# Attention into mixture-of-experts on one core: list operands by nine token tiles, wider routing steps, later weight rounding, and a sooner split of every second pair's outputs

## The chip, the cores and the metric

The kernel runs on 1 core of one Trainium2 chip, in one launch. The metric is device time in microseconds. Before the change it is 1155.81 us, the median of three runs (1155.4 to 1158.08).

## The reference

```
# q, k, v: 8 batches x 8 heads x 1152 x 64; q is averaged over pairs of positions -> 576 queries
q_pool = q.reshape(B, H, S // 2, 2, D).mean(axis=3)
scores = (1 / sqrt(D)) * q_pool @ k^T           # 576 x 1152 for each head
attn   = softmax(scores)                        # row maxima subtracted
x      = (attn @ v), heads side by side         # 4608 tokens x 512
logits = x @ w_gate + modality_bias[modality_id]        # 8 experts
e_idx  = argmax(logits);  gate = softmax(logits)[e_idx] # one expert for each token
out[t] = gate[t] * (relu(x[t] @ w1[e]) @ w2[e])         # 512 -> 1024 -> 512
```

All inputs and outputs are f32. The kernel splits f32 values into a high and a low 16-bit part and sums the products of the parts.

## The kernel before, in words

**Pairs.** The 64 heads are taken as 32 pairs (two batches of one head index, 128 partitions). `attention` runs 32 x 18 steps; `now[0]` is the step, and a pair's steps are its places 0 to 17. The order of TensorE, ScalarE, VectorE and GpSimd is the order of issue, written out by hand: in each step the letters of `ORD` advance generators for scores (`s`), value products (`v`) and the maxima of the next pair (`M`, `X`), `J` advances the logits' generators and `F` runs what `later(n, ...)` put off by n steps; `ends(t)` then runs what `later_end` and `go`/`at` put at the step's end. SyncE's queue, which issues most DMAs, is ordered by the scheduler of the framework instead.

**A pair's path.** `load_kq`, `split_q`, `split_qh`, `split_hi`, `split_lo` bring q and k of a pair two pairs ahead and split them (GpSimd and ScalarE). `maxpass` multiplies q and k (L778, L786), VectorE reduces each bank to maxima (L779, L787) out of three banks; at the end VectorE makes the row's maxima `m` (L749), TensorE turns them (L753), VectorE writes `mr` (L762), and a DMA (L763) puts `mr` into row 64 of `B2`. The scores' second matmul (L844) reads `B2`. ScalarE exponentiates each of four tiles of a unit (L845); the low words of the exponentials are made in two pieces, columns 0 to 1152 on ScalarE (L826) and 1152 to 1728 on VectorE (L828), as the `LOWS` tables say ('A' ScalarE, 'D' VectorE). Value products (L896 to L898) add into one bank for each head, and `evac` (L914 to L919) empties it; the second head's is emptied at place 4 of the next pair.

**Splitting the outputs.** `evac` then puts off `split_x` by `XD` = 5 steps (place 9): ScalarE makes `xh` (L862). `XL` = 3 steps later (place 12) VectorE makes `xl` (L872). For every second pair (odd p) a DMA transpose of two pairs' columns is issued after each (L880, SyncE), and the logits' job is put on a list that is looked at at place 8.

**Routing.** Nine token tiles of 128 (two batches, 8 pairs) are a group; there are four. When a group's logits are summed, `route` runs as the generator at the head of `side`, one piece at a time: the number that it yields is the number of steps to the next piece. It finds the maximum, the expert, the gate and each token's position within its expert. Groups 0, 1 and 2 are routed from pairs 9, 17 and 25 on, group 3 beside the experts.

**First list.** After group 2, `first_list` plans the six first blocks of 256 tokens (`first_blocks`), finds each token's place (`place`) and makes the list of tokens for each block by matmuls of one-hot operands (`operands`, `listing`, `indices`). At step 557, just before pair 31, `early` drains what is left of it, gathers the first block's tokens (GpSimd) and loads its weights; `T_W0` and `T_W1` say at which places of pair 31 the four pieces are loaded and rounded (L1432).

**Experts.** 18 blocks of 256 tokens and one of 128: two matmul stages with weights split into high and low parts. `beside()` advances group 3's logits, its `route` and `other_list` once for each twelfth or sixth matmul, whatever they yield; sixteen times a block. After block 4 the rest is drained.

Of the kernel before, what the change touches and what calls it, by code (L numbers as in the profile page):

```python
# [42 lines left out]
T_LIST = -127  # L43
RS = 2
SLOW_P = 1
# [72 lines left out]
W1D = 0  # L118
T_W1 = (6, 4, 10, 11)
E1 = 1  # L120
# [40 lines left out]
class Router:  # L161
# [11 lines left out]
    def setup(self, ids, w_gate, bias):  # L173
# [20 lines left out]
        nc.gpsimd.memset(self.on, 1.0)  # L194
        self.ie = self.iota("ie", E)
        self.lane16 = con.tile([P, P], BF16, name="lane16")
        nc.gpsimd.tensor_copy(self.lane16, self.iota("lane", P))
# [75 lines left out]
    def route(self, g, eng):  # L273

        nc, sm = self.nc, self.sm
        while self.added[g] < H // 2:
# [15 lines left out]
        yield RS + 1  # L292
# [16 lines left out]
        yield RS  # L309
# [11 lines left out]
        eng.dma_start(out=self.xs[g * NT * P:(g + 1) * NT * P, DM:XW].rearrange("(t p) d -> p t d", p=P), in_=gt)  # L321
        yield RS
# [3 lines left out]
        nc.tensor.matmul(pr[:, 0:NT], self.up, oh16, start=True, stop=False, skip_group_check=True)  # L326
        for s in range(NT):
            nc.tensor.matmul(pr[:, s + 1:], self.on, oh16[:, s:s + 1].broadcast_to([P, NT - s, E]), start=False, stop=s == NT - 1,
                             skip_group_check=True)
# [5 lines left out]
        self.base = nb  # L335
        yield RS
        nc.gpsimd.tensor_tensor(pos, pos, oh, op=ALU.mult)
        yield RS
        nc.vector.tensor_reduce(self.pos[:, ts], pos, op=ALU.add, axis=AX.X)
# [29 lines left out]
    def first_blocks(self):  # L369

        nc, sm = self.nc, self.sm
        full = self.con.tile([P, E], F32, name="full")
        self.up_to(self.base, full)
        yield
        cum = self.running(full.unsqueeze(1), "cumA")[:, 0]
        yield
        left = sm.tile([P, E], F32, name="left")
        nc.vector.tensor_scalar(left, cum[:, 0:E], -1.0, float(NA), op0=ALU.mult, op1=ALU.add)
        nc.vector.tensor_single_scalar(left, left, 0.0, op=ALU.max)
        self.na = self.con.tile([P, E], F32, name="na")  # L380
        nc.vector.tensor_tensor(self.na, full, left, op=ALU.min)
        yield
        nc.vector.tensor_single_scalar(cum, cum, float(NA), op=ALU.min)
        self.cumA = cum
        yield
        self.ownA = self.owners(cum, NA, "A")

# [37 lines left out]
    def place(self, nt, late):  # L425
# [11 lines left out]
        def pick(o, of):  # L437

            nc.vector.tensor_tensor(w, oh, be(of), op=ALU.mult)
            yield  # L440
            nc.vector.tensor_reduce(o, w, op=ALU.add, axis=AX.X)
            nc.vector.tensor_single_scalar(o, o, float(TB), op=ALU.mult)
            yield
# [5 lines left out]
        if late:  # L449
            yield from pick(ok, self.done)  # L450
            nc.vector.tensor_tensor(ok, self.pos[:, 0:nt], ok, op=ALU.is_ge)
            more = new("more")
            yield from pick(more, self.half)
            nc.vector.tensor_tensor(more, more, ok, op=ALU.mult)
            nc.vector.tensor_tensor(row, row, more, op=ALU.add)
        yield
        nc.vector.tensor_tensor(ok, self.pos[:, 0:nt], lim, op=ALU.is_ge if late else ALU.is_lt)
# [4 lines left out]
        lo = sm.tile([P, NTT], I32, name="loi")[:, 0:nt]  # L462
        nc.vector.tensor_single_scalar(lo, ri, P - 1, op=ALU.bitwise_and)
        nc.vector.tensor_single_scalar(ri, ri, 7, op=ALU.logical_shift_right)
# [3 lines left out]
        nc.vector.tensor_copy(self.hi, ri)  # L468
        nc.vector.tensor_single_scalar(self.hi, self.hi, -float(2 * T // P), op=ALU.add)

    def operands(self, g, n, out):

        nc, sm = self.nc, self.sm
        for q in range(3):
            ts = slice(g * NT + 3 * q, g * NT + 3 * q + 3)
            ol = sm.tile([P, 3, P], BF16, name=f"ol{q}", bufs=1 + self.lag)
            nc.vector.tensor_tensor(ol, self.lo[:, ts].unsqueeze(2).broadcast_to([P, 3, P]), self.lane16.unsqueeze(1).broadcast_to([P, 3, P]),
                                    op=ALU.is_equal)
# [3 lines left out]
            nc.vector.tensor_tensor(o, self.hi[:, ts].unsqueeze(2).broadcast_to([P, 3, n]), self.col[:, 0:n].unsqueeze(1).broadcast_to([P, 3, n]),  # L482
                                    op=ALU.is_equal)
            nc.vector.tensor_tensor(r[:, :, 0], o, self.tile1[:, ts].unsqueeze(2).broadcast_to([P, 3, n]), op=ALU.mult)
            nc.vector.tensor_scalar(r[:, :, 1], o, self.part, None, op0=ALU.mult)
            out.append((ol, r))
            yield SLOW

    def listing(self, groups, n, acc):

        nc, ops = self.nc, []
        for g in range(groups + self.lag):
            if g < groups:
                ops.append([])
                yield from self.operands(g, n, ops[g])
            elif self.lag:
                for _ in range(self.ll):
                    yield
            g -= self.lag
            if g >= 0:  # L500
                pm = self.pm(4)[:, 0:2 * n].rearrange("p (w n) -> p w n", w=2)
                for t in range(NT):
                    ol, r = ops[g][t // 3]
                    nc.tensor.matmul(pm, ol[:, t % 3], r[:, t % 3], start=t == 0, stop=t == NT - 1)
# [40 lines left out]
def attention(tc, ctx, att, ident, npairs, xpool, on_two, on_split, on_scale, jobs, side, set_pm, started, ahead, hip):  # L545
# [260 lines left out]
    def scores(p, j, r):  # L806
# [9 lines left out]
        s["P", j, r] = (word(F16, 1), Pl, i % NR)  # L816
        lows = LOWS_LAST if p == npairs - 1 else LOWS_LIST if p >= P_LIST else LOWS if p else LOWS0
        lows = lows[i % len(lows)]
# [86 lines left out]
    def evac(p, j, xp):  # L905
# [585 lines left out]
```

## Time and profile before

| | |
|---|---|
| median of the runs | 1155.81 us |
| profiled execution, its time | 1161.75 us |
| its span | 1160.0 us |
| granted TensorE clock, mean | 0.992 of full speed |
| TensorE busy | 1108.3 us (96%) |
| VectorE busy | 983.8 us (85%) |
| ScalarE busy | 920.6 us (79%) |
| GpSimd busy | 414.1 us (36%) |

The attention stage fills about the first 754 us, the experts the rest. A busy TensorE is not TensorE at its peak, since matmuls overlap and their ends are modelled; so lengths of equal pieces of work, and waits, are compared. In the tables of waits a line reads: engine, what waited and its line, what released it, then the sum in us, how often, and the longest. In a timeline a line gives the start, the length, the engine, the line, the operation, out<-in with shapes, how many are merged, and in brackets the idle time before it and what ended that.

### The profile page before, as it was taken

To read this page: it belongs to the slowest core of one execution; us is meant where nothing else is said; L and a number is where in the kernel's file an instruction comes from. 1 tells how busy PE (TensorE), PEld (TensorE's weight loads), DVE (VectorE), ACT (ScalarE), POOL (GpSimd) and SP (SyncE) were. 2 spreads that over 40 slices of the span, in tenths; PEclk is the share of its full clock that TensorE was granted. 3 is DMA by queue.
4 is the path that set the end of the run, shared out by engine and by line. 5 is a ranking of instruction groups with operands and counts; after the bars stand their busy time and mean duration, and the time that the engine had idled before them with its cause. 6 is when DMAs were issued, how large, how long until landed. Compare 5 with 4: busy or idle time off the path is not lost. (4 is left out here: it accounts for less than half of the span.)

```text
span 1160.0 us, 36631 instructions
## 1 busy us (share of the span) xinstructions
PE 1108.3 (96%) x14963; PEld 814.4 (70%) x14963; DVE 983.8 (85%) x2023; ACT 920.6 (79%) x1469; POOL 414.1 (36%) x394
## 2 busy tenths in 40 slices
PE   5999999999999999999999999899999999999995
PEld 2777777777777777777777677767676676666763
DVE  6999999999999999999999999688987667566661
ACT  5999999989999998999999999766656656565561
POOL 7853434444443444435344441123112221211211
PEclk8999999999999999999999999999999999999998
DMA  7766867866868768668678463699899999999980
GB/s 227 203 174 164 185 166 166 190 168 165 174 160 203 162 165 192 158 164 188 173 160 185 131 142 82 178 275 275 260 278 297 300 268 274 277 286 279 264 239 22
DMA packets 175569, 232.66 MB, mean 201 GB/s; under 512 B 92351, under 2 KB 126799, under 8 KB 175392
## 3 DMA queue, kind: packets, MB, share of 16 engines
q1 hardware_dynamic: 169254, 210.45, 70.3%
q0 software_dynamic: 6128, 19.78, 6.3%
q8 instruction: 119, 1.95, 0.7%
q14 instruction: 58, 0.48, 0.1%
q10 hardware_dynamic: 10, 0.00, 0.0%
HBM read 146.11 MB, written 19.18 MB: 142 GB/s over the span
## 5 line engine op out<-in xcount | busy, mean ns | idle before, releaser
L845 ACT ACTIVATE Pe<-psc 128x432 int32<-128x432 f32 x768 | 379.3, 526 | 49.9 <-PE psc L844 40.6
L779 DVE TENSOR_REDUCE mp<-pm 128x1 f32<-128x512 f32 x566 | 372.8, 684 | 23.3 <-PE pm L778 17.0
L896 PE MATMUL xp<-VH,Pe 128*128 128x65 f16 x2880 | 372.8, 194 | 0.0
L898 PE MATMUL xp<-VS,Pl 128*128 128x65 f16 x2880 | 372.2, 193 | 0.4 <-DVE Pl L828 0.4
L897 PE MATMUL xp<-vl,Pe 128*128 128x64 f16 x2880 | 371.0, 192 | 0.0
L897 PEld LDWEIGHTS <-Pe 128*128 128x128 f16 x2880 | 267.9, 98 | 87.6 <-issue 0.2
L844 PE MATMUL psc<-B 65*128 65x432 f16 (+2 forms) x1152 | 306.0, 288 | 8.9 <-DMA B<-mr 8.9
L896 PEld LDWEIGHTS <-Pe 128*128 128x128 f16 x2880 | 272.2, 98 | 54.8 <-issue 17.7
L843 PE MATMUL psc<-B 128*128 128x432 f16 (+2 forms) x1152 | 305.5, 287 | 3.4 <-ACT Pe L845 3.1
L898 PEld LDWEIGHTS <-Pl 128*128 128x128 f16 x2880 | 266.7, 97 | 0.6 <-DVE Pl L828 0.5
L826 ACT ACTIVATE Pl<-Pe 128x1152 f16<-128x1152 uint16 x196 | 223.3, 1140 | 6.2
L778 PE MATMUL pm<-hi,QB 128*128 128x512 f16 x566 | 214.6, 381 | 9.4 <-DVE mp L779 8.8
L731 POOL TENSOR_SCALAR VH<-rawv,sc 128x512 f16<-128x512 f32 (+1 forms) x60 | 103.5, 1735 | 173.9 <-PE psc L844 76.8
L644 POOL TENSOR_TENSOR lo<-rawk,hi 128x576 f16<-128x576 f32 (+1 forms) x68 | 87.6, 1291 | 186.3 <-ACT hi L628 147.4
L1230 PE MATMUL ph<-xpart,w1h 128*128 128x256 f16 x544 | 148.3, 273 | 0.1
L1232 PE MATMUL ph<-xpart,w1l 128*128 128x256 f16 x544 | 148.3, 273 | 0.0
L1231 PE MATMUL ph<-xpart,w1h 128*128 128x256 f16 x544 | 148.3, 273 | 0.0
L844 PEld LDWEIGHTS <-B 65*128 65x128 f16 x1152 | 113.3, 98 | 29.3 <-issue 5.1
L843 PEld LDWEIGHTS <-B 128*128 128x128 f16 x1152 | 113.0, 98 | 9.3 <-issue 4.0
L1236 DVE SCALAR_TENSOR_TENSOR hl<-ph,hh 128x512 f16<-128x512 f32 x72 | 49.6, 689 | 77.9 <-ACT hh L1235 62.3
L1235 ACT ACTIVATE hh<-ph 128x512 f16<-128x512 f32 x72 | 43.0, 597 | 88.5 <-PE ph L1232 80.3
L1278 PE MATMUL po<-w2h,hl 128*128 128x512 f16 x296 | 112.2, 379 | 0.0
(264 smaller groups left out, 1909.2 us busy)
## 6 DMA issues: line engine op xcount, KB each, us to landing
w2r<-in_w_dram SPq DMA_DIRECT2D x76, 512.0 KB
w1r<-in_w_dram SPq DMA_DIRECT2D x72, 512.0 KB
rawv<-in_att_dram SPq DMA_DIRECT2D x32, 576.0 KB
B<-hi SPq DMA_DIRECT2D x128, 144.0 KB
rawq<-in_att_dram SPq DMA_DIRECT2D x31, 576.0 KB
rawk<-in_att_dram SPq DMA_DIRECT2D x31, 576.0 KB
B<-qh SPq DMA_DIRECT2D x128, 72.0 KB
B<-lo SPq DMA_DIRECT2D x64, 144.0 KB
```

Source lines behind the costliest of these rows:

```text
L778: nc.tensor.matmul(pm, QB[p % 2][:, u], s["hi"][:, t * 512:(t + 1) * 512], start=True, stop=True)
L779: nc.vector.tensor_reduce(mp[:, u, t:t + 1], pm, op=ALU.max, axis=AX.X)
L826: nc.scalar.activation(low, rest, AF.Copy, scale=LOW)
L843: nc.tensor.matmul(o, b1[:, ks], b1[:, qs], start=True, stop=False, skip_group_check=True)
L844: nc.tensor.matmul(o, b2[:, ks], b2[:, qs], start=False, stop=True, skip_group_check=True)
L845: nc.scalar.activation(Pe[:, D + x0:D + x1], pt, AF.Exp, scale=1.0 / 16)
L896: nc.tensor.matmul(out, Ph[:, qs], vh[:, c, j, 0:D + 1], start=c == 0 and g == 0, stop=False, skip_group_check=True)
L897: nc.tensor.matmul(out[:, 0:D], Ph[:, qs], vl[:, c, j], start=False, stop=False, skip_group_check=True)
L898: nc.tensor.matmul(out, Pl[:, qs], vs[:, c, j, 0:D + 1], start=False, stop=c == NKC - 1, skip_group_check=True)
L1230: nc.tensor.matmul(o, hi[:, c, fs], xh[:, :, c], start=c == 0, stop=False)
L1231: nc.tensor.matmul(o, hi[:, c, fs], xl[:, :, c], start=False, stop=False)
L1232: nc.tensor.matmul(o, lo[:, c, fs], xh[:, :, c], start=False, stop=c == 3)
```

## The change

It has five parts. The split of an odd pair's outputs is put off by 2 steps instead of 5, for all but the last pair. `route` yields `RS[g]` steps (4, 4, 2, 2) instead of 2, three single steps are added to it, the expert's key is made in one operation with a table shifted by -8 (`ieE`), the one-hot is written as bf16 only, and three small operations go from VectorE to GpSimd. `first_blocks` and `place` are cut into more pieces, with one step between pieces in `first_blocks` and `PL` = 2 in `place`, and the multiplication by the block's size is fused. The operands of a list are made for a group of nine tiles in five pieces instead of three times two. The low words of pairs 28 to 30 are made on VectorE again where one in three was on ScalarE. The first two weight pieces of the first block are rounded at places 7 and 6 instead of 6 and 4.

```diff
-RS = 2
+PL = 2
+RS = (4, 4, 2, 2)
-P_LIST = 26
-LOWS_LIST = (((0, 1152, 'A', 2), (1152, 1728, 'D', 3)), ((0, 1152, 'A', 2), (1152, 1728, 'D', 3)), ((0, 1152, 'A', 2), (1152, 1728, 'A', 3)))
+P_LIST = {26: 0, 27: 0}
+LOWS_LIST = [tuple(((0, 1152, 'A', 2), (1152, 1728, e, 3)) for e in x) for x in ('DDA', 'DA', 'A')]
-T_W1 = (6, 4, 10, 11)
+T_W1 = (7, 6, 10, 11)
...
     def route(self, g, eng):
...
-        yield RS
+        yield rs
         nc.scalar.activation(w, lg, AF.Exp)
-        nc.vector.tensor_single_scalar(w2, lg, 0.0, op=ALU.is_ge)
         key = big[1][:, 0]
-        nc.vector.scalar_tensor_tensor(key, w2, -float(E), be(self.ie), op0=ALU.mult, op1=ALU.add)
+        nc.vector.scalar_tensor_tensor(key, lg, 0.0, be(self.ieE), op0=ALU.is_ge, op1=ALU.mult)
         kmin = sm.tile([P, NT], F32, name="kmin")
         nc.vector.tensor_reduce(kmin, key, op=ALU.min, axis=AX.X)
-        yield RS
-        oh = big[1][:, 1]
+        yield rs
+        oh = sm.tile([P, NT, E], BF16, name="oh16")
         nc.vector.tensor_tensor(oh, key, bc(kmin), op=ALU.is_equal)
-        oh16 = sm.tile([P, NT, E], BF16, name="oh16")
-        nc.vector.tensor_copy(oh16, oh)
-        nc.vector.tensor_single_scalar(self.exp[:, ts], kmin, float(E), op=ALU.add)
-        yield RS
+        yield 1
+        nc.gpsimd.tensor_scalar(self.exp[:, ts], kmin, float(E), None, op0=ALU.add)
+        yield rs
         sx = sm.tile([P, NT], F32, name="sx")
         nc.vector.tensor_reduce(sx, w, op=ALU.add, axis=AX.X)
-        nc.vector.tensor_single_scalar(sx, sx, EPS, op=ALU.add)
...
         nc.vector.tensor_reduce(ts2[:, 0:1], self.scales[g].bitcast(F32), op=ALU.max, axis=AX.X)
-        nc.vector.tensor_single_scalar(ts2[:, 0:1], ts2[:, 0:1], 1.0 / XSC, op=ALU.mult)
+        yield 1
+        nc.gpsimd.tensor_scalar(sx, sx, EPS, None, op0=ALU.add)
+        nc.gpsimd.tensor_scalar(ts2[:, 0:1], ts2[:, 0:1], 1.0 / XSC, None, op0=ALU.mult)
+        yield 1
         nc.vector.reciprocal(ts2[:, 1:2], ts2[:, 0:1])
...
     def operands(self, g, n, out):
-        for q in range(3):
-            ts = slice(g * NT + 3 * q, g * NT + 3 * q + 3)
-            ol = sm.tile([P, 3, P], BF16, name=f"ol{q}", bufs=1 + self.lag)
...
-            yield SLOW
-            o = sm.tile([P, 3, n], F32, name=f"o{n}")
-            r = sm.tile([P, 3, 2, n], BF16, name=f"r{n}_{q}", bufs=1 + self.lag)
...
+        ts = slice(g * NT, (g + 1) * NT)
+        r = sm.tile([P, 2, NT, n], BF16, name=f"r{n}", bufs=1 + self.lag)
+        ols = [sm.tile([P, 3, P], BF16, name=f"ol{q}", bufs=1 + self.lag) for q in range(3)]
...
+        rows(0)
+        yield SLOW
+        o = sm.tile([P, NT, n], F32, name=f"o{n}")
+        nc.vector.tensor_tensor(o, self.hi[:, ts].unsqueeze(2).broadcast_to([P, NT, n]), self.col[:, 0:n].unsqueeze(1).broadcast_to([P, NT, n]),
+                                op=ALU.is_equal)
+        yield SLOW
+        rows(1)
+        yield SLOW
+        nc.vector.tensor_tensor(r[:, 0], o, self.tile1[:, ts].unsqueeze(2).broadcast_to([P, NT, n]), op=ALU.mult)
+        nc.vector.tensor_scalar(r[:, 1], o, self.part, None, op0=ALU.mult)
+        yield SLOW
+        rows(2)
+        yield SLOW
...
     def first_list(self):
         for _ in self.first_blocks():
-            yield 2
+            yield 1
         for _ in self.place(3 * NT, False):
-            yield 2
+            yield PL
...
-            later(XD, lambda: split_x(p, x2))
+            later(2 if p % 2 and p < npairs - 1 else XD, lambda: split_x(p, x2))
```

## Rows read from the trace of the kernel before

**Rows 1.** Waits of TensorE, the whole span.

```profile
PE psc L844 <- DMA B<-mr: 8.9, 10, 1.6
PE pm L778 <- DVE mp L779: 8.8, 15, 1.1
```

**Rows 2.** Windows by pair, 9, 10, 14, 15, 26 to 29; columns: PE, PEld, DVE, ACT, POOL.

```profile
232.33:256.95 24.62, 23.62 (x416) 18.28 (x415) 23.98 (x64) 22.24 (x38) 10.71 (x14) 1.00 0.62 167
256.95:278.74 21.79, 20.95 (x357) 16.09 (x355) 20.88 (x48) 20.09 (x35) 10.46 (x9) 1.00 0.80 174
...
346.55:367.51 20.96, 20.95 (x360) 16.18 (x359) 20.20 (x45) 19.98 (x36) 9.04 (x7) 1.00 0.90 202
367.51:390.48 22.97, 22.97 (x404) 17.77 (x403) 22.00 (x48) 21.82 (x37) 9.78 (x9) 1.00 0.55 149
...
618.14:640.05 21.91, 21.48 (x367) 16.51 (x365) 21.39 (x60) 20.96 (x37) 10.91 (x10) 1.00 0.84 187
640.05:666.80 26.75, 24.41 (x409) 18.37 (x406) 26.15 (x65) 24.06 (x40) 9.52 (x8) 1.00 0.48 130
666.80:689.24 22.44, 21.03 (x361) 16.20 (x359) 22.05 (x55) 21.25 (x37) 9.84 (x8) 1.00 0.73 146
689.24:713.24 24.00, 22.99 (x400) 17.64 (x399) 23.37 (x56) 22.44 (x38) 7.95 (x6) 1.00 0.35 89
```

**Rows 3.** Timeline of SyncE's queue in pair 20.

```profile
487.64 5.91 SPq L880 DMA_TRANSPOSE xt<-x  x2
493.65 0.80 SPq L763 DMA_DIRECT2D B<-mr  x1
```

**Rows 4.** Timeline of VectorE in pair 20.

```profile
490.37 0.27 DVE L762 TENSOR_SCALAR mr<-pm 9x128 f16<-9x128 f32 x1
```

**Rows 5.** Timeline of TensorE at the starts of pairs 0 and 21.

```profile
18.01 0.52 PE L844 MATMUL psc<-B 65*128 65x432 f16 x1 [1.14 <-DMA B<-mr]
...
497.63 0.34 PE L844 MATMUL psc<-B 65*128 65x432 f16 x1 [1.56 <-DMA B<-mr]
```

**Rows 6.** Timeline of VectorE in pair 14, places 11 and 12.

```profile
354.32 0.18 DVE L749 TENSOR_REDUCE m<-mp 128x9 f32<-128x27 f32 x1
354.42 0.81 DVE L872 SCALAR_TENSOR_TENSOR x<-x,sc,x 128x576 f16<-128x576 f32 x1
355.14 0.45 DVE L828 TENSOR_SCALAR Pl<-Pe 128x576 f16<-128x576 uint16 x1
```

**Rows 7.** Timeline of TensorE in pair 14.

```profile
354.57 0.27 PE L753 MATMUL pm<-ident,m 128*9 128x128 f32 x1
```

**Rows 8.** Timeline of GpSimd in pair 14.

```profile
350.87 1.60 POOL L644 TENSOR_TENSOR lo<-rawk,hi 128x576 f16<-128x576 f32 x1 [2.68 <-ACT hi L628]
```

**Rows 9.** Timelines of VectorE and of GpSimd in pair 25.

```profile
613.36 0.63 DVE L305 TENSOR_TENSOR wide<-wide,kmin 128x72 f32<-128x72 f32 x1
...
613.22 1.56 POOL L731 TENSOR_SCALAR VH<-rawv,sc 128x512 f16<-128x512 f32 x1 [6.17 <-PE pm L778]
```

**Rows 10.** Groups by line and shape, VectorE: the lists' operands; busy us, mean ns.

```profile
L477 DVE TENSOR_TENSOR ol<-lof,lane 128x384 bf16<-128x384 bf16 x21 | 11.6, 550 | 0.0
...
L485 DVE TENSOR_SCALAR r<-o,part 128x114 bf16<-128x114 f32 x12 | 3.9, 325 | 0.0
...
L482 DVE TENSOR_TENSOR o<-hif,col 128x114 f32<-128x114 f32 x12 | 3.3, 272 | 0.0
L485 DVE TENSOR_SCALAR r<-o,part 128x36 bf16<-128x36 f32 x9 | 2.2, 243 | 0.0
...
L482 DVE TENSOR_TENSOR o<-hif,col 128x36 f32<-128x36 f32 x9 | 1.7, 187 | 0.0
```

**Rows 11.** The same view: the low words on VectorE.

```profile
L828 DVE TENSOR_SCALAR Pl<-Pe 128x576 f16<-128x576 uint16 x176 | 91.8, 522 | 2.7 <-ACT Pe L845 1.4
```

**Rows 12.** Timeline of ScalarE in pair 31.

```profile
735.98 1.06 ACT L1432 ACTIVATE w1h<-rawk 128x1024 f16<-128x1024 f32 x1 [2.48 <-DMA rawk<-in_w_dram]
```

**Rows 13.** Timeline of TensorE in pair 31.

```profile
737.51 0.28 PE L843 MATMUL psc<-B 128*128 128x288 f16 x1 [2.22 <-ACT Pe L845]
```

More of the change, by code (lines that the diff above doesn't have):

```diff
@@ L195, in setup @@
         self.ie = self.iota("ie", E)
+        self.ieE = self.iota("ieE", E, base=-E)
         self.lane16 = con.tile([P, P], BF16, name="lane16")
@@ L273, in route @@
     def route(self, g, eng):
-        nc, sm = self.nc, self.sm
+        nc, sm, rs = self.nc, self.sm, RS[g]
         while self.added[g] < H // 2:
@@ L289, in route @@
         nc.gpsimd.tensor_tensor(w, w, w2, op=ALU.add)
-        yield RS
+        yield rs
         nc.gpsimd.tensor_tensor(lg, lg, w, op=ALU.add)
-        yield RS + 1
+        yield rs + 1
         mx = sm.tile([P, NT], F32, name="mx")
@@ L321, in route @@
         eng.dma_start(out=self.xs[g * NT * P:(g + 1) * NT * P, DM:XW].rearrange("(t p) d -> p t d", p=P), in_=gt)
-        yield RS
+        yield rs
         for _ in range(self.ll - 1):
@@ L325, in route @@
         pr = self.pm(4)[:, 0:(NT + 1) * E].rearrange("p (t e) -> p t e", e=E)
-        nc.tensor.matmul(pr[:, 0:NT], self.up, oh16, start=True, stop=False, skip_group_check=True)
+        nc.tensor.matmul(pr[:, 0:NT], self.up, oh, start=True, stop=False, skip_group_check=True)
         for s in range(NT):
-            nc.tensor.matmul(pr[:, s + 1:], self.on, oh16[:, s:s + 1].broadcast_to([P, NT - s, E]), start=False, stop=s == NT - 1,
+            nc.tensor.matmul(pr[:, s + 1:], self.on, oh[:, s:s + 1].broadcast_to([P, NT - s, E]), start=False, stop=s == NT - 1,
                              skip_group_check=True)
@@ L335, in route @@
         self.base = nb
-        yield RS
+        yield rs
         nc.gpsimd.tensor_tensor(pos, pos, oh, op=ALU.mult)
-        yield RS
+        yield rs
         nc.vector.tensor_reduce(self.pos[:, ts], pos, op=ALU.add, axis=AX.X)
@@ L372, in first_blocks @@
         full = self.con.tile([P, E], F32, name="full")
-        self.up_to(self.base, full)
+        i = sm.tile([P, E], I32, name="cnti")
+        nc.vector.tensor_copy(i, self.base)
         yield
-        cum = self.running(full.unsqueeze(1), "cumA")[:, 0]
+        nc.vector.tensor_single_scalar(i, i, TB.bit_length() - 1, op=ALU.logical_shift_right)
+        yield
+        nc.vector.tensor_copy(full, i)
+        yield
+        w = sm.tile([P, 1, E + 1, E], F32, name="wcumA")
+        nc.vector.tensor_tensor(w[:, 0], full.unsqueeze(1).broadcast_to([P, E + 1, E]), self.before, op=ALU.mult)
+        yield
+        cum = self.con.tile([P, E + 1], F32, name="cumA")
+        nc.vector.tensor_reduce(cum, w[:, 0], op=ALU.add, axis=AX.X)
         yield
@@ L378, in first_blocks @@
         nc.vector.tensor_scalar(left, cum[:, 0:E], -1.0, float(NA), op0=ALU.mult, op1=ALU.add)
+        yield
+        cut = self.con.tile([P, E + 1], F32, name="cutA")
         nc.vector.tensor_single_scalar(left, left, 0.0, op=ALU.max)
+        nc.vector.tensor_single_scalar(cut, cum, float(NA), op=ALU.min)
+        self.cumA = cut
+        yield
         self.na = self.con.tile([P, E], F32, name="na")
         nc.vector.tensor_tensor(self.na, full, left, op=ALU.min)
+        c3 = sm.tile([P, NA, E], F32, name="own3A")
+        nc.vector.tensor_tensor(c3, self.col[:, 0:NA].unsqueeze(2).broadcast_to([P, NA, E]), cut[:, 1:].unsqueeze(1).broadcast_to([P, NA, E]), op=ALU.is_ge)
         yield
-        nc.vector.tensor_single_scalar(cum, cum, float(NA), op=ALU.min)
-        self.cumA = cum
+        ef = sm.tile([P, NA], F32, name="ownA")
+        nc.vector.tensor_reduce(ef, c3, op=ALU.add, axis=AX.X)
         yield
-        self.ownA = self.owners(cum, NA, "A")
+        self.ownA = self.con.tile([P, NA], I32, name="ownerA")
+        nc.vector.tensor_single_scalar(self.ownA, ef, float(E - 1), op=ALU.min)
     def other_blocks(self):
@@ L455, in place @@
             nc.vector.tensor_tensor(row, row, more, op=ALU.add)
+        nc.vector.tensor_tensor(ok, self.pos[:, 0:nt], lim, op=ALU.is_ge if late else ALU.is_lt)
         yield
-        nc.vector.tensor_tensor(ok, self.pos[:, 0:nt], lim, op=ALU.is_ge if late else ALU.is_lt)
         nc.vector.scalar_tensor_tensor(row, row, float(2 * T), ok, op0=ALU.add, op1=ALU.mult)
@@ L461, in place @@
         nc.vector.tensor_copy(ri, row)
-        lo = sm.tile([P, NTT], I32, name="loi")[:, 0:nt]
+        yield
+        lo, hi = (sm.tile([P, NTT], I32, name=f"{x}i")[:, 0:nt] for x in ("lo", "hi"))
         nc.vector.tensor_single_scalar(lo, ri, P - 1, op=ALU.bitwise_and)
-        nc.vector.tensor_single_scalar(ri, ri, 7, op=ALU.logical_shift_right)
+        nc.vector.tensor_single_scalar(hi, ri, 7, op=ALU.logical_shift_right)
+        yield
         self.lo = sm.tile([P, NTT], BF16, name="lof")[:, 0:nt]
@@ L467, in place @@
         self.hi = sm.tile([P, NTT], F32, name="hif")[:, 0:nt]
-        nc.vector.tensor_copy(self.hi, ri)
+        nc.vector.tensor_copy(self.hi, hi)
+        yield
         nc.vector.tensor_single_scalar(self.hi, self.hi, -float(2 * T // P), op=ALU.add)
@@ L473, in operands, with rows @@
         nc, sm = self.nc, self.sm
-        for q in range(3):
-            ts = slice(g * NT + 3 * q, g * NT + 3 * q + 3)
-            ol = sm.tile([P, 3, P], BF16, name=f"ol{q}", bufs=1 + self.lag)
-            nc.vector.tensor_tensor(ol, self.lo[:, ts].unsqueeze(2).broadcast_to([P, 3, P]), self.lane16.unsqueeze(1).broadcast_to([P, 3, P]),
-                                    op=ALU.is_equal)
-            yield SLOW
-            o = sm.tile([P, 3, n], F32, name=f"o{n}")
-            r = sm.tile([P, 3, 2, n], BF16, name=f"r{n}_{q}", bufs=1 + self.lag)
[L482 to L487, printed above, removed]
+        ts = slice(g * NT, (g + 1) * NT)
+        r = sm.tile([P, 2, NT, n], BF16, name=f"r{n}", bufs=1 + self.lag)
+        ols = [sm.tile([P, 3, P], BF16, name=f"ol{q}", bufs=1 + self.lag) for q in range(3)]
+        out.append((ols, r))
+        def rows(q):
+            t3 = slice(g * NT + 3 * q, g * NT + 3 * q + 3)
+            nc.vector.tensor_tensor(ols[q], self.lo[:, t3].unsqueeze(2).broadcast_to([P, 3, P]), self.lane16.unsqueeze(1).broadcast_to([P, 3, P]),
+                                    op=ALU.is_equal)
+        rows(0)
[11 more added lines that the diff above has]
+        yield SLOW
     def listing(self, groups, n, acc):
@@ L502, in listing @@
                 for t in range(NT):
-                    ol, r = ops[g][t // 3]
-                    nc.tensor.matmul(pm, ol[:, t % 3], r[:, t % 3], start=t == 0, stop=t == NT - 1)
+                    ols, r = ops[g][0]
+                    nc.tensor.matmul(pm, ols[t // 3][:, t % 3], r[:, :, t], start=t == 0, stop=t == NT - 1)
                 yield 1
```

7 lines of the change are left out of this document (3 added, 4 removed).

## The prediction, made before the changed kernel was built

> **What bounds the kernel now.** I read the waits of TensorE first, because the page gives that engine as busy for 96% of the span: a change can only earn what is left in its waits and in stretches that another engine paces. Two waits matter [rows 1]. Ten times, 8.9 us in all, a scores matmul (L844) waits for the DMA that brings the row of maxima `mr` into B2; 1.1 us of that is pair 0's start [rows 5], so nine waits in steady state are worth 7.8 us. Fifteen times, 8.8 us in all, a maxima matmul (L778) waits for VectorE to empty its bank.
>
> Then I cut the attention stage into pairs, from the second emptying of an output (L914; place 4 of the next pair's 18 steps) to the next one [rows 2]. Where nothing is waited for, an even pair takes 20.96 us (pair 14) and an odd one, which carries the logits, 22.97 us (pair 15). VectorE is busy 20.20 and 22.00 us of these, ScalarE 19.98 and 21.82: three engines are within 5% of each other, so what is moved counts, not only what is removed. Pair 9, with a group's routing, takes 24.62 us, and pair 10 after it 21.79. The first list costs pair 26 21.91, pair 27 26.75, pair 28 22.44 and pair 29 24.00 us; in these VectorE is busy all but half a microsecond. So the excess over quiet pairs is 1.65 + 0.83 us for each of the three routings (the third one's second part lies in pair 26), and 0.95 + 3.78 + 1.48 + 1.03 us for the list.
>
> **Part 1, every second pair's outputs split three steps sooner.** An odd pair's outputs are split in the next, even pair: ScalarE makes `xh` at place 9, VectorE `xl` at place 12, and SyncE issues a transpose after each. In pair 20 the two transposes hold SyncE from 487.64 to 493.55 [rows 3]; `mr` was written by 490.64 [rows 4], its DMA is issued at 493.65, and TensorE waits 1.56 us for it [rows 5]. Three steps are some 3.7 us (20.96 us over 18 steps, times 3). With both transposes that much sooner SyncE is free at about 490 to 491.5, `mr` goes 2 us or more sooner, and all nine waits go: -7.8 us. The other DMAs that the transposes pass on SyncE's queue (the next pair's loads, the moves of qh) are not waited for in any row.
>
> What is late next: `xl` moves ahead of the row's maxima on VectorE. In pair 14 the order is maximum `m` (L749) at 354.32, `xl` at 354.42, the next operation at 355.14: `xl` takes 0.72 us of the queue [rows 6]. `m` ends at 354.50, and TensorE's transposition of it (L753) starts at 354.57 without having waited [rows 7]. With `xl` in front, `m` ends 0.72 us later and L753 stands for about 0.7 us, with everything queued behind it on TensorE: value products, then scores. VectorE has no idle time in that half of the pair to swallow it (busy 20.20 of 20.96). ScalarE's `xh` comes before the half of `hi` at place 7 and makes three exponentials late; with three score banks I allow 0.2 us for that, and in the likeliest case it lies inside the 0.7. In the ten even pairs from 2 to 24 without a routing I therefore take -7.8 + 10 x 0.71 = -0.7 us. Bounds: -7.8 (the hold is swallowed) and, with the hold and ScalarE's 0.2 on top, +1.3.
>
> **Part 2, routing spaced wider.** Sixteen more VectorE instructions stand in pair 9 than in pair 15, 1.98 us of busy time [rows 2], so 0.12 us each. Five are removed: the comparison is fused into the key, the one-hot is written once as bf16, and three small operations go to GpSimd. With four steps between the pieces for groups 0 and 1, pair 9 keeps three (the reduction of the logits, the maximum, the difference); the other eight fall into pair 10, three of them before its `m`. Pair 9 falls to about 23.0: -1.6. Pair 10 then has the 0.7 us hold of part 1, and before `m` the key, its minimum and the one-hot, 0.36 us at 0.12 each and 0.9 if the one-hot takes the 0.63 us of today's L305 [rows 9]; I take 0.8. Against the 0.83 that it loses today: +0.7. For two groups 2 x (-1.6 + 0.7) = -1.8 us; bounds -4.9 (both excesses gone) and +0.5.
>
> The reciprocals now wait for two small GpSimd operations issued one step before. GpSimd's queue holds the halves of `lo` (1.60 us, [rows 8]) at places 10 and 13 and VH at places 3 and 4; by the order of issue none of these ends later than a step ahead, so I cost the hand-over at nothing. If that cover is gone, VectorE stands for up to one such operation, 1.6 us, four times; the maxima queue behind it and TensorE behind them. That is inside the bound of the range above.
>
> A rule bears on the moved operations. The one-hot comparison L305 took 0.63 us in pair 25, from 613.36, while GpSimd was in a 1.56 us operation begun at 613.22 [rows 9], and it ended before that one did. The Trainium skill (SBUF — State Buffer, Who interferes with whom) says that a VectorE instruction with two SBUF inputs is blocked until a reading GpSimd instruction ends. By the rule L305 would have stood until 614.78, so the row shows less; what the rule would do to `xl` is the third rival below.
>
> **Part 3, the first list by nine tiles.** By the order of issue, extra VectorE instructions in pairs 25 to 29 go from 16, 16, 19, 12, 9 (72) to 6, 18, 11, 10, 7 (52): the list starts ten steps later (step 514, not 504), but a group takes fifteen steps, not eighteen. The o operation goes from 187 ns for 36 elements to 272 ns for 114, the last one from 243 to 325 [rows 10]; at 108 elements a group costs about 0.27 + 0.27 + 0.32 where three of 0.19 + 0.20 + 0.24 stood, so 1.0 us less busy time a group. But the low words of pairs 28 to 30 come back from ScalarE to VectorE, two of 0.52 us (mean) in each pair [rows 11].
>
> Pair 25: ten instructions fewer, -1.6, down to the quiet length. Pair 26: about as many; its floor is 20.96 + 0.7 (part 1's hold): -0.2. Pair 27: 26.15 - 22.00 = 4.15 us of extra VectorE time today; eight instructions fewer, among them an `ol` of 0.55 us and an operand triple, leave about 1.3: -3.0. Pair 28: one `ol` and two triples fewer (0.55 + 1.0), o and r in one piece and two low words more: -0.3, mostly because pair 27 hands on less delay. Pair 29: four `ol` for two (+1.1), two low words more (+1.0), two triples and the accumulation fewer (-1.5): with little idle time there, +0.9. Pair 30: `xl` and the low words ahead of its last `m`, and a larger remainder when the list is drained at step 557 (r, r and ol for one triple): +0.5. Sum -3.7 us; bounds -8.9 (all excess of pairs 25 to 29 gone) and +1.0 (the low words take back pair 27's gain).
>
> **Part 4, the first block's weights.** In pair 31 ScalarE reaches the rounding of `w1h` one step after the third load is issued and stands 2.48 us for the data [rows 12]; TensorE then waits 2.22 us for exponentials [rows 13]. Two steps later is 2.3 us, so ScalarE does the exponentials first and the data is there: -2.0 us. Bounds -2.2 and, if the load lands later too, 0. The order of the two roundings stays, and the later ones' places don't move.
>
> **The experts.** Route 3 takes three more slots, placing three more, the list four fewer: it ends two slots later, at 76 of 80, and still before the drain after block 4. TensorE is busy without a gap there, so 0; bounds -0.5 and +0.5.
>
> **Sum.** -0.7 - 1.8 - 3.7 - 2.0 = -8.2 us. The profiled execution took 1161.75 us, its span 1160.0; both lie 4 to 6 us over the median 1155.81. The terms are waits inside pairs, so I take them off the median whole: 1147.6, say **1148 us**.
>
> **Rivals.** *A: the hold does not appear.* `mr`'s waits go and VectorE has `m` ready: for it, pair 30's stretch is short of work and part 2 frees VectorE; against it, 0.07 us of slack at L753. Twelve holds of 0.7 us fewer: 1148 - 8 = 1140 us. Chance 0.15.
>
> *B: the list gains nothing.* What pair 27 loses comes back in 28 to 30 through the low words, and pair 26 takes what 25 sheds. For it: VectorE is the pacing engine in all five pairs, and the moved work stays on it. Against it: twenty instructions are gone. Part 3 at 0 to +1 instead of -3.7: 1152 us. Chance 0.22.
>
> *C, slower: the sooner `xl` collides.* ScalarE's `xh` delays `hi`, so GpSimd's `lo` (1.60 us from 350.87, [rows 8]) moves by 0.6 us to end at about 353.1, just where `xl` wants to start (353.04). If `xl`, reading two SBUF tiles, is held by `lo` for that 0.6 us, each of fifteen even pairs stands 1.3 us, 19.7 us against the 7.8 saved: +11.9, and with the other parts' -7.5 it is 1160 us. It decides from a hold of some 1.02 us a pair ((7.8 + 7.5) / 15). The skill's rule above speaks for it. Against it: L305 was not held to the end. Chance 0.13.
>
> **How the numbers follow.** My case has 0.50, with 1144 to 1152.5 as its own range. A measurement of this kernel tells 0.3%, 3.5 us, from no change: the line is 1152.3 below and 1159.3 above. Faster: 0.47 of my case, all of A, a quarter of B: 0.67. Slower: C's larger half: 0.08. The rest, 0.25, is no change. The range reaches into A and down B's side: 1140 to 1156.
>
> **What would show it.** L844's waits for `mr` gone from pair 2 on, and L753 waiting for `m` about ten times, 0.7 us each: part 1 as argued; no such waits is A; 1.2 us and more is C. Pair 9 at 23.0 and pair 10 above 22: part 2. Pair 27 near 24 and pair 29 near 25: part 3; their sum unchanged is B. ScalarE's wait for the data of `w1h` under 0.5 us: part 4. If even pairs take 20.96 us throughout, the prediction is wrong on the slow side.

## The result and the profile after

| | before | changed |
|---|---|---|
| median of 20 runs each, one chip | 1155.44 us | 1157.63 us |
| ratio, 95% interval | | 1.0026 [1.0017, 1.0035] |
| profiled execution | 1161.75 us | 1156.40 us |
| its span | 1160.0 us | 1154.6 us |
| its mean granted clock | 0.992 | 0.996 |

The change costs 0.26%, some 3 us, where 8 were to be won. It lies inside the 0.3% that counts as no change, and outside the range. The two profiles say the opposite of the runs: the one before is longer than each of that kernel's 20 runs (1152.75 to 1160.14), the one after is the shortest of its 20. So a difference between these two traces is not the difference between the kernels; lengths of pairs that several executions agree on are used below. Lines of `attention` stand 30 higher in the changed kernel (L844 is L874, L753 is L783, L914 is L944).

Waits of TensorE after the change, columns as in [rows 1]:

```profile
PE pm L783 <- DVE m L779: 9.8, 14, 1.3
...
PE psc L874 <- DMA B<-mr: 2.2, 5, 0.7
```

The waits for `mr` have shrunk, and the waits by the transposition of the maxima (L783) have grown to 9.8 us. I call them holds. Before, the same line read:

```profile
PE pm L753 <- DVE m L749: 2.1, 5, 0.7
```

The windows of pairs 9, 10, 14, 15 and 26 to 29, columns as in [rows 2]; the number ahead of the DMA share is the granted clock:

```profile
232.21:255.18 22.97, 22.97 (x404) 17.78 (x403) 22.35 (x52) 21.82 (x37) 11.46 (x14) 1.00 0.59 160
255.18:277.72 22.54, 21.49 (x371) 16.60 (x370) 21.42 (x55) 20.75 (x37) 10.39 (x11) 1.00 0.81 188
344.97:366.35 21.38, 20.89 (x360) 16.23 (x359) 19.93 (x45) 20.20 (x36) 8.74 (x7) 1.00 0.98 200
366.35:389.32 22.97, 22.97 (x404) 17.78 (x403) 22.00 (x49) 21.82 (x37) 9.78 (x9) 1.00 0.57 156
...
613.66:637.05 23.39, 21.87 (x379) 17.00 (x378) 22.46 (x61) 21.80 (x38) 10.73 (x11) 1.00 0.90 194
637.05:662.23 25.18, 23.68 (x399) 17.86 (x398) 24.84 (x57) 23.23 (x39) 9.78 (x9) 1.00 0.47 132
662.23:686.05 23.82, 21.03 (x359) 16.20 (x358) 22.95 (x55) 20.51 (x35) 8.94 (x7) 1.00 0.69 135
686.05:711.26 25.21, 23.60 (x413) 18.10 (x412) 24.90 (x55) 22.41 (x37) 8.32 (x7) 1.00 0.35 88
```

Pairs 9 and 10 are as forecast (23.0; above 22). Pair 27 lost 1.57 us, but 26, 28 and 29 gained 1.48, 1.38 and 1.21.

SyncE's queue in pair 20, with what stands ahead of the transpositions; it answers to [rows 3]:

```profile
480.67 0.53 SPq L629 DMA_DIRECT2D rawv<-in_att_dram  x1
481.30 0.39 SPq L624 DMA_DIRECT2D rawq<-in_att_dram  x1
481.79 0.38 SPq L228 DMA_DIRECT2D xs<-x  x1
482.26 5.73 SPq L910 DMA_TRANSPOSE xt<-x  x1
488.09 0.54 SPq L609 DMA_DIRECT2D B<-qh  x1
488.72 2.00 SPq L910 DMA_TRANSPOSE xt<-x  x1
490.81 0.79 SPq L793 DMA_DIRECT2D B<-mr  x1
```

The first transposition starts sooner and lasts 5.73 us. Measured from the start of the pair (479.17) it runs from 3.1 to 8.8; before the change the pair's transpositions began at 6.2. Three transfers of 576 KB (the load of v, the load of q, the store of x2) are issued in the 1.6 us ahead of it.

VectorE in the same pair, the rows that answer to [rows 6]:

```profile
485.65 0.81 DVE L902 SCALAR_TENSOR_TENSOR x<-x,sc,x 128x576 f16<-128x576 f32 x1
...
487.67 0.18 DVE L779 TENSOR_REDUCE m<-mp 128x9 f32<-128x27 f32 x1
```

And TensorE, answering to [rows 5, 7]:

```profile
487.91 0.28 PE L783 MATMUL pm<-ident,m 128*9 128x128 f32 x1 [0.48 <-DVE m L779]
...
494.98 0.34 PE L874 MATMUL psc<-B 65*128 65x432 f16 x1 [0.55 <-DMA B<-mr]
```

`xl` (L902) now stands ahead of the row's maxima, the transposition waits 0.48 us for them, and the wait for `mr` is still there, since its DMA left 2.3 us after `mr` was written (488.50). Six other even pairs show the same 0.48 to 0.49.

### The profile page after: what moved, and what is told of

It reads as the page before. It is cut to its first block, busy times and chain, and to the rows that moved or that the text cites. A ratio compares the mean times of both kernels' runs of the same rounds, so it can differ in the third digit from the quotient of the medians.

```text
span 1154.6 us, 36573 instructions
## 1 busy us (share of the span) xinstructions
PE 1106.6 (96%) x14963; PEld 813.5 (70%) x14963; DVE 977.6 (85%) x1961; ACT 919.1 (80%) x1463; POOL 417.0 (36%) x408
## 5 line engine op out<-in xcount | busy, mean ns | idle before, releaser
L874 PE MATMUL psc<-B 65*128 65x432 f16 (+2 forms) x1152 | 305.7, 288 | 2.2 <-DMA B<-mr 2.2
L856 ACT ACTIVATE Pl<-Pe 128x1152 f16<-128x1152 uint16 (+1 forms) x190 | 219.2, 1154 | 6.0
L874 PEld LDWEIGHTS <-B 65*128 65x128 f16 x1152 | 113.2, 98 | 24.7 <-issue 2.1
L1307 PE MATMUL po<-w2l,hh 128*128 128x512 f16 x296 | 112.3, 379 | 0.0
```

The costliest lines, as they stand in the source:

```text
L856: nc.scalar.activation(low, rest, AF.Copy, scale=LOW)
L874: nc.tensor.matmul(o, b2[:, ks], b2[:, qs], start=False, stop=True, skip_group_check=True)
```

## Experiments

Each ratio is to the kernel before, run beside it on the same chip (its medians were 1155.2 to 1160.7 us, so ratios are compared); 0.1% is 1.16 us. The sum of pairs 25 to 30 is called the list stretch: 140.13 and 140.25 us in two executions of the kernel before, 140.63 in the changed one.

**1. The kernel before, profiled again.** No edit.

> The kernel before, unchanged, profiled a second time. Theory H (the sooner split costs more than it saves): the waits for the row of maxima that the first profile showed, 7.8 us in nine pairs, are larger than in a usual run, because that execution, 1161.75 us, lies above every one of its 20 plain runs; I expect 2 to 6 us here, an execution of 1153 to 1157 us, and pair 31 at about 17.5 us instead of 19.91 with no lowered granted clock there. Theory L (the list is the loss): the waits for the row of maxima are 7 to 9 us again and only the ends of the attention stage (pair 0, pair 31) differ.

Ratio 0.9999 [0.9982, 1.0015], profiled execution 1160.59 us. Its waits of TensorE:

```profile
PE psc L844 <- DMA B<-mr: 10.3, 10, 1.5
...
PE pm L753 <- DVE m L749: 2.2, 5, 0.8
```

Its window of pair 31:

```profile
735.36:751.95 16.59, 15.74 (x332) 13.63 (x331) 14.80 (x32) 14.27 (x27) 2.67 (x2) 1.00 0.49 165
```

The same window in the first profile of this kernel:

```profile
733.63:753.55 19.92, 17.18 (x333) 14.60 (x331) 14.87 (x31) 14.32 (x27) 2.67 (x2) 0.91 0.42 147
```

Theory H's first half is wrong here: the waits for `mr` are 10.3 us, in an execution near the median of its chip (1160.73 us). They aren't the same everywhere, though. On the chip of experiments 8 to 10, where the kernel before takes 1155.24 us, the two profiled kernels that keep the old split and the old store (the weights alone, the routing alone) show less:

```profile
PE psc L844 <- DMA B<-mr: 6.8, 8, 1.6
...
PE psc L845 <- DMA B<-mr: 3.4, 5, 1.0
```

Pair 31 is 3.3 us shorter: the 2.22 us wait of [rows 13] and the lowered clock after it belong to that one execution. In every other trace a scores matmul waits at most 0.6 us for exponentials.

**2. The sooner split alone, and the change without it.**

```diff
-            later(XD, lambda: split_x(p, x2))
+            later(2 if p % 2 and p < npairs - 1 else XD, lambda: split_x(p, x2))
```

This edit in the kernel before is only_split; its reverse in the changed kernel is split_back.

> The kernel before with the sooner split of odd pairs' outputs and nothing else. Theory H: twelve to fifteen holds of the transposition of the maxima, 0.5 us and more each, 6 to 9 us, against 2 to 6 us of saved waits: 2 to 5 us slower than the kernel before. Theory L: the split alone is a gain, 0 to 4 us faster, as the prediction's term of -0.7 has it.

> The changed kernel with the split put back to five steps in all pairs. Theory H: 3 to 6 us faster than the changed kernel, so 1152 to 1155 us and faster than the kernel before. Theory L: no faster than the changed kernel, 1157 to 1159 us, since the loss is in pairs 26, 28 and 29.

only_split: 1.0044 [1.0023, 1.0065]. split_back: 0.9985 [0.9967, 1.0003]. Both ways the sooner split costs 0.41 to 0.44%, 4.7 to 5.1 us, each with some 0.2% of uncertainty: theory H holds in its size. That split_back is faster than the kernel before, as H had it, is not shown. The 0.41% compares ratios taken beside two medians of the kernel before, 1155.44 and 1160.73 us. Beside the same runs, the kernel of experiment 3, which differs from split_back by the split and the low words, is 0.24% slower than it. Waits of TensorE with the split alone:

```profile
PE pm L753 <- DVE m L749: 9.4, 14, 1.3
...
PE psc L844 <- DMA B<-mr: 5.5, 7, 1.7
```

Against experiment 1, 4.8 us of waits for `mr` went and 7.2 us of holds came. In these two traces pair 31 ends 5.9 us later. The larger part, 3.8 us, is in the list stretch, 144.08 us; its pair 28 ran at a granted clock of 0.93, so a part of that may be this execution's. The seven even pairs without routing or list from 8 on (8, 12, 14, 16, 20, 22 and 24, called quiet) lose 0.4 us together, and pairs 10 and 18, where a routing's VectorE work goes on, 1.3 us.

**3. The low words on ScalarE again.**

```diff
-P_LIST = {26: 0, 27: 0}
+P_LIST = 26          # and LOWS_LIST of the kernel before
```

> The changed kernel with the tables of the low words as in the kernel before (one in three on ScalarE from pair 27 on). Theory H: within 1 us of the changed kernel. Theory L: pairs 26, 28 and 29 lose the 1.2 to 1.5 us each that they gained in length, 2 to 4 us faster than the changed kernel.

1.0009 [0.9994, 1.0024], not told apart from the changed kernel's 1.0026: 2 us faster, give or take 2, which alone doesn't rule out the low end of theory L. The list stretch took 140.32 us, 0.3 less, and by that L falls: the low words are not where the list's gain went.

**4. Only the first transposition sooner.** xh three steps sooner, xl kept at place 12.

```diff
-        later(XL, lambda: split_xl(p, x2))
+        later(XL + 3 if p % 2 and p < npairs - 1 else XL, lambda: split_xl(p, x2))
```

> The kernel before with the first half of the split (xh and its transposition) three steps sooner, while xl stays at place 12. Theory Q (SyncE is held by the three 576 KB transfers issued just ahead of the first transposition, so that a sooner start gains nothing, and the holds come from xl in front of the row's maxima): the first transposition takes 4 to 6 us and ends where it does in the kernel before, about 9 us after the pair's start; no holds of the transposition of the maxima; 8 to 11 us of waits for mr; within 0.2% of the kernel before. Rival R (the sooner first transposition does clear the queue, and only xl spoils it): waits for mr under 4 us, no holds, 5 to 7 us faster.

1.0014 [0.9996, 1.0032]. Waits of TensorE:

```profile
PE psc L844 <- DMA B<-mr: 10.4, 10, 1.9
...
PE pm L753 <- DVE m L749: 1.8, 3, 0.7
```

SyncE's queue in pair 20, which starts at 480.88:

```profile
483.96 5.64 SPq L880 DMA_TRANSPOSE xt<-x  x1
489.69 0.54 SPq L579 DMA_DIRECT2D B<-qh  x1
490.33 2.11 SPq L880 DMA_TRANSPOSE xt<-x  x1
492.54 0.80 SPq L763 DMA_DIRECT2D B<-mr  x1
```

Rival R falls. Over seven quiet even pairs the first transposition began at 3.66 us of the pair and ended at 8.82; in experiment 1 it began at 6.24 and ended at 9.06. 2.6 us sooner in, 0.24 us sooner out; the holds are gone with `xl` back in its place.

**5. Two transfers off SyncE's queue.** The kernel before, the store of x2 (12 steps after the last emptying) and even pairs' load of v issued by GpSimd; every load of v also comes two steps later (`T_LV`).

```diff
-T_LV = -24
+T_LV = -22
-        eng.dma_start(out=self.xs[...], in_=x2)
+        self.nc.gpsimd.dma_start(out=self.xs[...], in_=x2)      # put off by later(12, ...)
-        nc.sync.dma_start(out=t, in_=att[p, :, 2 * S:3 * S])
+        (nc.gpsimd if p > 2 and p % 2 == 0 else nc.sync).dma_start(out=t, in_=att[p, :, 2 * S:3 * S])
```

> The kernel before, its split at the old places, with two of the three 576 KB transfers that stand ahead of the transpositions in even pairs (the store of x2 and the load of v) issued by GpSimd after its last lo of the pair instead of by SyncE. Theory Q: the first transposition takes under 2 us, from 6.2 to about 8 us after the pair's start, the second follows xl at 8.7 and ends by 10.3, mr's DMA leaves at 10.2 to 10.5 instead of 12.1, and the waits for mr fall from about 10 us to under 3: 5 to 8 us faster than the kernel before, less what a late v costs. Rival R (a transposition is long by itself or through another engine): the two transpositions still hold SyncE for 5 us and the time stays within 2 us.

0.9999 [0.9989, 1.001]. The queue did what theory Q says: the first transposition takes 1.3 us (6.24 to 7.56 in pair 14), `mr` leaves at 10.1, its waits are 1.4 us in 2. The gain went, at least in part, to the late v: a matmul at L696 waits 6.1 us in 9 for ScalarE's squares of v, a wait that the kernel before doesn't have. The end of the program gave 3.9 us back (see 10), so the pairs lost about as much.

**6. Only the store moved.** As 5 without the load of v.

> As the kernel with both transfers moved, but with the store of x2 alone issued by GpSimd. Theory Q: a third of the bytes ahead of the transpositions is gone, so the first one ends 1 to 2 us sooner and the waits for mr fall by about half: 3 to 6 us faster than the kernel before. Rival R: no change within 2 us.

0.9977 [0.9952, 1.0001], 2.7 us, less than expected and not quite told from none. It is no more than what the end of the program gives back (2.75 us, see 10), so the pairs gained nothing. The first transposition takes 1.3 to 2.1 us, `mr` is waited for twice (3.4 us, 2.3 of it in pair 6). But quiet even pairs take 21.6 us instead of 20.96: GpSimd issues the store for 1.06 us just ahead of the addition of the next q. In 9 and 10 it stands behind that.

**7. The list one step later.** The changed kernel with one line more at the head of `first_list`:

```diff
+        yield 1
         for _ in self.first_blocks():
```

> The changed kernel with the planning of the first list started one step later, and nothing else. Theory G (VectorE instructions that begin while GpSimd is in a two-input operation stand until that ends: the cast L376 took 1.24 us for 8 elements, L458 1.43 where its twin took 0.37, L405 0.60): a step later most of these fall beside GpSimd's operation, they take 0.16, 0.37 and 0.2 us, and pairs 26 to 27 together get 1.5 to 3 us shorter; 1 to 3 us faster than the changed kernel. Rival V (the sum of VectorE's work sets these pairs and holds only fill slack): pairs 25 to 30 together stay within 0.7 us of the changed kernel's 140.6.

1.0011 [0.9995, 1.0027]; list stretch 141.12. In the changed kernel, the timelines of VectorE and of GpSimd around the cast L376:

```profile
626.24 1.24 DVE L376 CAST cnti<-base 128x8 int32<-128x8 f32 x1
...
626.04 1.41 POOL L639 TENSOR_TENSOR rawq<-rawq 128x576 f32<-128x576 f32 x1
```

The cast a step later, with GpSimd idle:

```profile
629.48 0.17 DVE L376 CAST cnti<-base 128x8 int32<-128x8 f32 x1
```

The durations are mostly G's: the cast 1.24 to 0.17 us, L405 0.60 to 0.16, L458 1.43 to 0.85 where G had 0.37. Pairs 26 and 27 got 0.8 us shorter where G had 1.5 to 3. The time is not G's: the stretch stayed within 0.5 us, as V has it (pair 28 ran at a granted clock of 0.93 here, so a part of the gain may hide behind that). The holds are shown, their price isn't.

**8. The routing alone, and the weights alone.** `route`, `RS` and `ieE` of the changed kernel in the kernel before; and `T_W1 = (7, 6, 10, 11)` in it.

> The kernel before with the wider spaced routing and its moved operations alone. Theory Q with the routing as predicted: pairs 9 and 17 fall to 22.97, pairs 10 and 18, without the sooner split's hold, come to 22.65, pair 25 falls by about 1.4 us: 2.5 to 3.5 us faster than the kernel before. Rival W (what leaves pair 25 comes back in pairs 26 and 27): 1 to 2 us faster.

> The kernel before with the first two roundings of the first block's weights later, and nothing else. By the second profile of the kernel before, whose pair 31 took 16.59 us and not 19.91, the 2.22 us wait that the prediction took away is not there in a usual run: within 1 us of the kernel before, pair 31 at 16.6 to 17.3. Rival (the prediction's term): 2 us faster.

The weights: 0.999 [0.9977, 1.0003], no difference, pair 31 at 17.01. The routing: 1.0037 [1.0023, 1.005], slower, though pairs 9 and 17 took 22.97, pairs 10 and 18 22.65 and pair 25 23.25. What it cost stands in the windows of pairs 26 and 27:

```profile
609.83:634.19 24.36, 21.97 (x377) 16.97 (x376) 22.82 (x61) 21.79 (x38) 10.53 (x11) 1.00 0.72 177
634.19:663.46 29.27, 24.65 (x408) 18.47 (x403) 28.67 (x66) 23.96 (x40) 11.76 (x10) 1.00 0.46 127
```

With [rows 2] that is 2.45 and 2.52 us more: group 2's routing ends later, the old list starts later, and its pieces pile up in pair 27 (VectorE busy 28.67 us). My expectation missed this, and rival W was far too mild.

**9. The routing and the store.** The kernel before with `route` as in 8 and the store of x2 on GpSimd behind the addition of q (`later(17, ...)`).

> The kernel before with the wider routing, and with the store of x2 issued by GpSimd, here after the addition of the next pair's q, where GpSimd stands idle for some 5 us. Theory Q: the waits for mr are gone (8 to 10 us), even quiet pairs take 20.96 us again and not 21.6, and the routing's 2.5 us come on top: 7 to 11 us faster than the kernel before. Rival W and a late store: 3 to 5 us faster.

**10. All but the sooner split, and the store.** The changed kernel with `later(XD, ...)` and that store.

> The changed kernel with its split put back to five steps and the store of x2 issued by GpSimd in the same place. If the list by nine tiles, the low words and the later weights are worth something together, this is faster than the one with the routing alone; by the sums of pairs 25 to 31 in the traces so far (142.2 + 17.1 with the list's change, 140.2 + 16.6 without) it is 1 to 3 us slower than that one, so 5 to 9 us faster than the kernel before.

9: 0.9954 [0.9941, 0.9967], 5.3 us faster than the kernel before, short of theory Q's 7 to 11. 10: 0.9918 [0.9905, 0.993], a median of 1145.77 us beside 1155.24, faster than both kernels. The order that I expected was wrong: with the routing in both, the list, the low words and the weights are worth 0.36%, 4.2 us; the list stretch is 145.12 us in 9 and 141.01 in 10. SyncE's queue in pair 20 of experiment 10:

```profile
476.71 0.53 SPq L629 DMA_DIRECT2D rawv<-in_att_dram  x1
477.34 0.40 SPq L624 DMA_DIRECT2D rawq<-in_att_dram  x1
478.37 0.47 SPq L609 DMA_DIRECT2D B<-qh  x1
481.44 3.71 SPq L910 DMA_TRANSPOSE xt<-x  x2
485.25 0.79 SPq L793 DMA_DIRECT2D B<-mr  x1
```

The windows of its pairs 14 and 20:

```profile
342.11:362.91 20.80, 20.80 (x360) 16.18 (x359) 20.12 (x46) 19.88 (x36) 10.06 (x8) 1.00 0.86 196
475.21:496.01 20.80, 20.80 (x360) 16.18 (x359) 20.12 (x46) 19.89 (x36) 10.06 (x8) 1.00 0.80 193
```

Its wait of TensorE for `mr`:

```profile
PE psc L874 <- DMA B<-mr: 0.6, 1, 0.6
```

All seven quiet even pairs take 20.79 or 20.80 us, less than the 20.96 that was the shortest in [rows 2]. Both transpositions together (3.71 us with `xl` between) end at 485.15, and `mr` leaves 0.8 us after it was written. Moving the store is worth 0.67% here against split_back and 0.83% in 9 against 8, 7.7 to 9.6 us. Not all of it comes from the waits for `mr`. When the program ends, GpSimd's queue runs a long drain; in experiments 1 and 9 (shortest, middle and longest of three, in ns; then first and last start):

```profile
L1486 POOLq DRAIN  x3: 40/107/6286, 1151.8 to 1158.6; - x3
...
L1487 POOLq DRAIN  x3: 40/107/4081, 1142.2 to 1146.9; - x3
```

The drain takes 6.29 us in all ten traces with the store on SyncE, 4.08 in experiments 6, 9 and 10, and 3.18 in 5. The instruction ahead of it (INC_SWDGE_SEM) falls from 1.72 us to 1.18, and to 0.96 in 5. Together that is 2.75 us, and 3.87 in 5; why, no run shows. So 5 to 7 us are left for the pairs, where the prediction hoped for 7.8.

Two things about the queue stay open. No record has the time at which the three transfers arrive, so that the transposition waits for them to drain is inferred: from when it is short, and from what the DMA engines move. In the seventh to ninth us of pair 20 that is 287 GB/s in the changed kernel, where the transposition runs until 8.8, and 128 in experiment 10 (the last number):

```profile
485.17:488.17 3.00, 2.52 (x52) 1.99 (x49) 2.96 (x7) 2.97 (x7) 0.04 (x1) 1.00 1.07 287
...
481.21:484.21 3.00, 3.00 (x59) 2.41 (x56) 2.96 (x8) 2.97 (x7) 0.00 (x0) 1.00 0.74 128
```

And every edit that moved the store to GpSimd's queue also issued it 12 or 17 steps later. A later store on SyncE was not run, so what the queue and what the time is worth is not parted.

## Why the prediction was wrong

**Part 1 failed.** The step is "With both transposes that much sooner SyncE is free at about 490 to 491.5, `mr` goes 2 us or more sooner, and all nine waits go: -7.8." It took the length of the transpositions as theirs. The first one, as far as the runs show, holds SyncE until the transfers issued ahead of it have drained: it ends at about the same time of the pair whether it starts at 3.7 or at 6.2 us (experiment 4), and it is short once one of the three is gone (6, 10). So `mr`'s DMA left 0.34 us sooner (11.74 us of the pair against 12.08, seven quiet pairs of 2 and of 1), and about half of the waits stayed (5.5 us with the split alone; 2.2 in the profile of the changed kernel). "The other DMAs that the transposes pass on SyncE's queue ... are not waited for" was the overlooked row: TensorE waits for none of them, but the transposition seems to. (The three steps are also 3.5 us, not 3.7: 20.96 / 18 x 3. The start moved by 2.6.) The hold of 0.71 us was of the right kind and 0.48 in quiet pairs, and the holds' growth of 7.2 us in experiment 2 is near the 7.1 of the sum; but there are 14 holds and not ten, up to 1.3 us long. Part 1 was put at -0.7 and is +4.7 to +5.1 us by runs. The waits that stayed are some 3 us of that; the rest lies mostly in the list stretch, where the sum allowed the split 0.7 us in pair 26 and a share of 0.5 in pair 30 (experiment 2: +3.8 us). Why it costs that much there stays open.

**Part 2 held for the groups it was worked out for.** Pairs 9, 10, 17 and 18 together took 92.82 us before and 91.03 after: -1.79, forecast -1.8. Nothing shows VectorE waiting for the operations handed to GpSimd. What it left out is group 2: Part 3 books pair 25's -1.6 and no return. By experiment 8 the return is 5 us in pairs 26 and 27, with the old list behind it.

**Part 3 failed in its sum.** -3.7 was forecast for pairs 25 to 30; they took +0.5 (140.13 to 140.63 us). Pair by pair: 25 and 27 -1.4 and -1.6 (forecast -1.6, -3.0); 26, 28, 29 and 30 +1.5, +1.4, +1.2 and -0.6 (forecast -0.2, -0.3, +0.9, +0.5). The nine-tile list does save about what I took, 4.2 us (9 against 10), but from a stretch that the routing had made 4.9 us longer. In the one trace of the changed kernel the sooner split takes nothing more there: 140.63 us with it, 141.01 without it (experiment 10). The price of one group's operands was nearly right: the sum took 0.20 us for the second of the three old operations, where the trace has 0.24. The busy time explains why counting instructions misled: with 18 VectorE instructions fewer, busy time rose from 133.3 to 134.4 us. The operands fell from 6.1 to 2.5 us, six low words came to VectorE for 0.5 us each, and instructions that met a GpSimd operation grew, as in experiment 7.

**Part 4 failed.** The step is the 2.22 us wait itself: [rows 12, 13] are true of the one profiled execution only. The edit is worth -0.10% [-0.23, +0.03].

**"I take them off the median whole"** is where that entered: the profile lay 4 to 6 us over the median, and 3.3 of these were in pair 31, in a wait that I then subtracted from a median that didn't contain it. The 7.8 us of waits for `mr` came out of the same execution; the five traces with the old split and the old store have 3.4 to 10.9 us of them.

**The rivals.** A didn't happen, the hold is there. B, the list gaining nothing, is what the stretch shows as a sum, though not through the low words. C had the sign right, but not the cause: `xl` was held by GpSimd's `lo` once, in pair 26 (1.28 us instead of 0.81, from 620.79, with `lo` from 620.17 to 621.45), but in the quiet pairs `lo` had ended before `xl` began.

By runs the sum is +5 (split), -1.2 ± 1.5 (weights), +4.2 (routing, with what it does to the old list), and the list and low words the rest to +3.0, about -5. That remainder is set by the sum and not measured; 9 against 10 has 4.2 us for the list, the low words and the weights together. That the parts add is not shown, since they were measured in different company.

## What to carry to other kernels

When a DMA instruction holds its queue, look at the bytes issued ahead of it before moving it: if it ends at the same time in pairs where it starts at different times, moving it does little, and moving one of the transfers ahead of it, which nobody else waits for, may do what was hoped for. Where parts of a change feed the same engine one after the other, price the end of the first as the start of the second. And subtract a wait from a median only if a second profile, or the other pairs of the same one, show it too.

## What the hardware showed that I had not expected

**A transposition that waits in its queue.** Over the seven quiet pairs the first transposition is 1.3 to 1.7 us long with two 576 KB transfers issued 3.9 to 4.7 us ahead of it (experiment 10), and 1.9 to 3.6 us with a third one 2.5 to 3.6 us ahead (experiment 1). In pair 20 of the changed kernel it is 5.7 us long with three issued in the 1.6 us ahead. The time is booked on the transposition, so that it looks slow itself.

**GpSimd's two-input operations hold VectorE.** L376, L405 and L902 (pair 26) began while GpSimd was in a `TENSOR_TENSOR`; the first two ended 0.03 us after it did, whatever they cost alone. With a `TENSOR_SCALAR` of GpSimd beside it the one-hot comparison took 0.63 us instead of 0.23 and ended before it ([rows 9]). The Trainium skill (SBUF — State Buffer, Who interferes with whom) says that a VectorE instruction in a two-port mode, which casts can use, or with two SBUF inputs shares ports with GpSimd, and that whoever issues first has them for the whole instruction while the other fully blocks. The cast agrees, 1.24 us instead of 0.17. The comparison, with two SBUF inputs, doesn't: 0.40 us of hold beside an operation of 1.56, as far as the profile's spans of GpSimd, which are rough, can be trusted. The prediction weighed the rule by the second case alone.

**The clock within the list stretch.** In split_back, 1 us slices of pair 26; the second number is TensorE's busy time, the third from the end the granted clock:

```profile
621.00:622.00 1.00, 0.42 (x15) 0.33 (x12) 0.96 (x6) 1.00 (x3) 0.42 (x2) 1.00 1.08 283
622.00:623.00 1.00, 0.52 (x9) 0.43 (x9) 1.00 (x2) 0.89 (x2) 0.91 (x2) 1.00 0.55 78
623.00:624.00 1.00, 0.54 (x6) 0.32 (x5) 1.00 (x3) 0.53 (x1) 1.00 (x1) 1.00 1.14 92
624.00:625.00 1.00, 1.00 (x15) 0.86 (x14) 1.00 (x3) 0.32 (x1) 1.00 (x2) 0.74 0.50 68
625.00:626.00 1.00, 1.00 (x8) 0.63 (x6) 0.22 (x3) 0.98 (x3) 0.86 (x2) 0.50 0.14 20
626.00:627.00 1.00, 1.00 (x18) 0.92 (x17) 0.68 (x1) 0.97 (x2) 0.00 (x0) 0.50 0.96 134
```

After three slices in which TensorE was half busy the clock stands at 0.50, the 1.2 GHz level, for about 3 us. The pair took 24.29 us; with the same list and no drop it took 22.95 (experiment 10). So in that execution the pile-up on VectorE cost TensorE twice, in waits and in clock. Whether it falls in a given execution stays open: in the changed kernel and in experiment 10 the same pair had the same two waits, 1.06 and 0.46 us, and kept its clock.
